# Convolution taps loaded by rows and turned on TensorE, four integer adds moved to GpSimd, and later landings written into the planner

## The chip, the cores and the metric

The kernel runs on one core of a Trainium2 chip. The metric is the device time of one execution in microseconds; the median of three runs stands for the kernel. All times, bytes and clocks below come from those runs and from one profiled execution.

## The reference

Chunked attention feeds a feed-forward block, and that feeds a gated convolution. All of it is computed to fp32 accuracy; the weights and the convolution taps arrive as 64-bit floats (two 32-bit words a number).

```python
# attention inside chunks of 64 tokens, B=8, H=8, S=576, D=64
scores = scale * q_c @ k_c.T;  attn = softmax(scores);  x = attn @ v_c     # -> x: 4608 tokens x 512
# feed-forward with layer norm, 512 -> 2048 -> 512
xn = (x - mu) / sqrt(var + 1e-6) * g_ln
x  = x + relu(xn @ w_ch1) @ w_ch2
# gate: a causal convolution over time with 5 taps a channel
gate_pre[t] = sum over k of conv_w[k] * x[t - 4 + k]
out = (sigmoid(gate_pre) * (x @ w_val)) @ w_out
```

## The kernel before

The 4608 tokens are cut into nine blocks of 512 (`NBLK`), each of four tiles of 128 (`unit(u)`: attention and layer norm of one tile). The feed-forward runs per block, over four groups of 512 hidden columns (`hidden(b, g)`; in the first two blocks `ffn`). Every fp32 product is made of three products of rounded halves (a "high" and a "low" part, the low one being what rounding left). From the third block on, a group is computed with seven products of half-size operands in place of eight (names "1" to "7", line 1241, TensorE tile `m`). The weight operands `late_a` of these are kept in HBM (`a_dram`) and loaded again for each block. At the end the value and output projections follow the same scheme (TensorE tiles `v` and `o`).

**Weights as 64-bit words.** `pieces` turns one or two 512 KB pieces of float64 words into fp32: ScalarE `f32_size` (line 297) and `f32_rest` (line 317), VectorE `f32_upper` (lines 302 and 305) and `f32_join` (line 320, an integer add of 128x1024 words for a pair), and then ScalarE's high part (line 384 or 388) and VectorE's low part (line 393 or 399). The first eight pieces are the weights of group 0. The taps of the convolution, 5 x 512 numbers, take the same route in `conv_taps`; their load reads eight bytes for each of 128 x 20 places, straight into channel-on-partition order.

**The convolution.** For each channel tile, ScalarE multiplies by tap 0 (line 1625, or 1568 for block 0, whose `x` is read back from HBM as `cx` or `late_x`), VectorE adds the other four taps (lines 1632, 1575), and SyncE stores the sum to `gate_dram` (lines 1645, 1587). The sums lie in two halves of `u_room`, so a third sum waits for the first one's store.

**Order of the work.** Nothing is scheduled by the compiler. Each piece of work is an `Op` with an engine, an assumed duration, dependencies and a priority; `Plan.run` plays these through a list scheduler when the kernel is built, and its order is the order in which every engine then executes. An op's result is assumed to be there after a hop, 3500 ns for a DMA, plus the op's own allowance `more`:

```python
HOP = {"PE": 220.0, "DVE": 80.0, "ACT": 80.0, "POOL": 200.0, "SP": 3500.0}
...
a.ready = max(a.ready, end + wait)     # wait holds HOP[e] + op.more
```

When TensorE has nothing ready in the planner's first 60 us, `keep_warm` puts in a 128x128 product of the identity (line 332, tiles `warm_h`, `warm_y`). These are instructions like others: they are executed whether or not the data has come by then. The planner counts 215 ns for one of them (430 ns before 7 us), and the trace shows each as two instructions. All DMAs go through SyncE's queue ("SP"), in planned order.

**Names used below.** `att` is a tile's attention bank on TensorE, `xnt` the turned, normalised tile (line 825 high, line 830 low), `h` and `hh`/`hl` the hidden values, `y` the second product of the feed-forward, `px`/`ps` the probabilities that a transposing DMA turns (line 676), `qT`/`kT` the turned q and k (line 561), `x7d` the operands stored for the value projection (line 1468), `rstd` a [128, 1] reciprocal root on GpSimd (line 756).

Of the kernel before, what the change touches and what calls it, by code (L numbers as in the profile page):

```python
# [18 lines left out]
P = 128  # L19
# [110 lines left out]
def chunk_attention_ffn_gated_conv(  # L130
# [157 lines left out]
    def words(ap):  # L288

        if len(ap.shape) == 3:  # L290
            w = ap.rearrange("p i (n w) -> p i n w", w=2)
            return w[:, :, :, 0], w[:, :, :, 1]
        w = ap.rearrange("p (n w) -> p n w", w=2)
        return w[:, :, 0], w[:, :, 1]
# [21 lines left out]
        lo = words(raw)[0]  # L316
        nc.scalar.activation(out=lo, in_=lo.bitcast(U32), func=AF.Copy, scale=2.0**-29)

    def f32_join(raw, u):
        nc.vector.tensor_tensor(out=u, in0=u, in1=words(raw)[0], op=ALU.add)  # L320

    npiece, uu_n = [0], [0]
    stage, spare = {}, {}
# [11 lines left out]
    def pieces(tags, srcs, pri, keep, dma_pri=None, scale=None, after=None, behind=None):  # L335
# [71 lines left out]
        o_size = add("ACT", 670 * n - 250 * (n - 1), size, [*loads, behind] + room_free, pri)  # L407
        o_rest = add("ACT", 670 * n - 250 * (n - 1), lambda: f32_rest(st["raw"]), [*loads, behind], pri)
        o_up = add("DVE", 1120 * n - 300 * (n - 1), lambda: f32_upper(st["raw"], st["u"]), [o_size], pri)
        o_join = add("DVE", 690 * n - 150 * (n - 1), lambda: f32_join(st["raw"], st["u"]), [o_up, o_rest], pri)  # L410
        if scale is None:
            o_high = add("ACT", 640 * n - 250 * (n - 1), high, [o_join, after], pri)
        else:
# [30 lines left out]
        hold("h0", c)  # L444
        return c

    def conv_taps(pri):

        st, n = {}, KT * KD

        def load():
            st["raw"] = slot("dg1", [P, 2 * n], I32, "cw_raw")
            nc.sync.dma_start(
                out=st["raw"].rearrange("p (n w) -> p n w", w=2),
                in_=conv_w.bitcast(I32).rearrange("k (f p w) -> p (k f) w", p=P, w=2),
            )

        def size():
            st["u"] = cw_sb.rearrange("p k f -> p (k f)").bitcast(I32)
            f32_size(st["raw"], st["u"])  # L460

        a = add("SP", 2000, load, [w_op[0, 2 * KD - 1]], pri)
        b = add("ACT", 200, size, [a], pri)
        c = add("ACT", 200, lambda: f32_rest(st["raw"]), [a], pri)
        d = add("DVE", 400, lambda: f32_upper(st["raw"], st["u"]), [b], pri)
        return add("DVE", 150, lambda: f32_join(st["raw"], st["u"]), [c, d], pri)


    def runs(t):
# [34 lines left out]
    def unit(u):  # L504
# [399 lines left out]
        if u < NT:  # L904
            room = take("qk") + take("uu1")
            early_pri = pri - STEP_TILE
            lq, lk = (
                op("SP", 2640 * len(runs(u)), load_blocks(i), room, p=early_pri) for i in range(2)
            )
            eq = op("DVE", 1110, turn(0), lq, take("A"))  # L910
            ek = op("DVE", 1110, turn(1), lk, take("B"))
            hold("qk", eq, ek)
            ready = [eq, ek]
# [7 lines left out]
        def turned_probabilities():  # L921
            sp = op("ACT", 1250, apart, ex, bu)
            cp = op("SP", 600, crossbar, sp, su, p=pri - 20000.0)
            cp.more = 1000.0
            return op("ACT", 1370, together, cp)

        ep = turned_probabilities() if ready else None
# [370 lines left out]
    def hidden(b, g):  # L1298
# [8 lines left out]
        def product(m, into, new, deps):  # L1307
            rt = RING[ring_n[0] % len(RING)]
            ring_n[0] += 1

            def load():
                w[m] = slot(rt, [P, 2, 2, two_f], F32R, f"a{b}_{g}_{m}")
                nc.sync.dma_start(out=w[m].bitcast(F32), in_=a_dram[g, m].bitcast(F32))

            def go():
                if new:
                    st[into] = bank(tb if into == "b" else ta, f"m{m}_{b}_{g}").rearrange("p (f x) -> p f x", f=2)
                x = operand(m)
                twelve(st[into], lambda s, k: w[m][:, s, k], lambda s, k: x[:, s, k], new)

            at = pri + 1400.0 * MS.index(m)
            ld = add("SP", 1300, load, [a_store[g, m]] + take(rt), at - 16000.0)
            ld.more = 1500.0
            o = add("PE", 1410, go, [ld, B_op[b, m]] + deps, at)
            hold(rt, o)
            if g == NG - 1:
                hold(f"o{m}", o)
            return o
# [228 lines left out]
    def conv_again(f):  # L1557
# [3 lines left out]
        def load():  # L1561
            st["x"] = slot(rt, [P, P0 + NB], F32, f"cx{f}")
            nc.sync.dma_start(out=st["x"][:, P0:], in_=x2_dram[:, f])
            nc.gpsimd.memset(st["x"][:, :P0], 0.0)

        def first():
            st["acc"] = slot(at, [P, XW], F32, f"acc0_{f}")
            nc.scalar.activation(
                out=st["acc"][:, :NB], in_=st["x"][:, :NB], func=AF.Copy, scale=cw_sb[:, 0, f : f + 1]
            )  # L1570
# [18 lines left out]
        pri = when[4 + f, KF // 2]  # L1589
        ox = add("SP", 1300, load, [x2_store[0]] + take(rt), pri - 8000.0)  # L1590
        ox.more = 2500.0
        oa = add("ACT", 740, first, [ox, cw_op] + take(at), pri)
        for i in range(1, KT):
            oa = add("DVE", 760, more(i), [oa], pri)
        hold(rt, oa)
        conv_store[0, f] = add("SP", 728, keep, [oa], pri)
        hold(at, conv_store[0, f])

    def conv(b):
# [19 lines left out]
        for f in range(KD if b else 0):  # L1619
# [31 lines left out]
                oa = add("DVE", 760, more(i), [oa], pri)  # L1651
            last.append(oa)
            conv_store[b, f] = add("SP", 728, keep, [oa], pri)
            hold(at, conv_store[b, f])
        if b == 0:
            x2_store[b] = add("SP", 2900, store, done, pri)
# [358 lines left out]


    g_op = ln_scale()
    for u in range(TB):
        unit(u)
    for g in range(NG):  # L2020
# [4 lines left out]
    for b, f in fstep:  # L2025
# [13 lines left out]
                weight_sums(f // 4)  # L2039
        elif f % 4 == 0:  # L2040
            hidden(b, f // 4)
        if (b, f) == (0, KF // 2 + 1):
            cw_op = conv_taps(when[0, 3 * KF // 4])
        if (b, f) == (NBLK - 1, KF - 4):
            val_weights()
            out_weights()
# [52 lines left out]
```

## Time and profile before

| | |
|---|---|
| three runs | 1072.77, 1078.07, 1076.52 us; median 1076.52 us |
| the profiled execution, its own time | 1073.77 us |
| its span, first to last instruction | 1072.0 us |
| TensorE / VectorE / ScalarE / GpSimd busy | 99% / 80% / 50% / 4% |
| mean granted TensorE clock | 0.998 of 2.4 GHz |
| HBM traffic over the span | 257 GB/s |

TensorE's ends are modelled, so its 99% hides short waits between products. In the first 48 us part of this busy time is the warm-up products.

### The profile page before, as it was taken

The page shows a single profiled execution, that of the slowest core. Times are in us where ns is not written, and L with a number is a line of the kernel's source. Part 1 is how long each engine was busy: PE and PEld are TensorE (multiplying, and loading weights), DVE is VectorE, ACT ScalarE, POOL GpSimd, SP SyncE. Part 2 cuts the span into 40 slices and gives each one's busy share as a digit, 9 for nine tenths or more (in the row PEclk, how much of TensorE's full clock was granted, in tenths as well). Part 3 has the DMA queues.
Part 4 walks back from the last instruction along what each step waited for, and adds up shares of the span by engine and source line. Part 5 has one row for each costly group of instructions (what it writes and reads, how often), then busy time and mean ns, then how long its engine had stood idle before and what let it go on. Part 6 is the DMA issues. An engine that isn't in the chain of part 4 may idle for free.

```text
span 1072.0 us, 22750 instructions
## 1 busy us (share of the span) xinstructions
PE 1056.9 (99%) x8953; PEld 953.9 (89%) x8953; DVE 857.1 (80%) x1463; ACT 539.0 (50%) x871; POOL 42.9 (4%) x81
## 2 busy tenths in 40 slices
PE   9999999999999999999999999999999999999998
PEld 8988878888999988889888889888999999999998
DVE  5989858888876888767888768778766889998785
ACT  5796534445454445444544543554453555655553
POOL 1011100000000000000000000000000000000000
PEclk9999999999999999999999999999999999999999
DMA  8996458666999899899999999899965988999952
GB/s 192 309 339 184 114 130 240 219 199 198 265 361 244 238 311 336 265 258 334 272 265 315 270 241 265 302 266 271 327 229 201 385 328 307 306 337 374 321 206 79
DMA packets 208451, 284.14 MB, mean 265 GB/s; under 512 B 101844, under 2 KB 153560, under 8 KB 208344
## 3 DMA queue, kind: packets, MB, share of 16 engines
q1 hardware_dynamic: 208344, 282.68, 85.1%
q8 instruction: 71, 1.16, 0.5%
q14 instruction: 36, 0.29, 0.1%
HBM read 207.64 MB, written 67.63 MB: 257 GB/s over the span
## 4 chain that ended last, share of the span: by engine, by line
PE 90%; DMA 4%; DVE 3%; ACT 1%; issue 1%; SPq 1%; POOL 0%; DVEq 0%; POOLq 0%; ACTq 0%
PE m L1241 22%; PE o L1241 8%; PE v L1241 8%; PE y L1020 7%; PE yA L1398 4%; PE yB L1398 4%; PE yA L1400 4%; PE yB L1400 4%; PE yA L1399 4%; PE yB L1399 4%; PE att L590 4%; PE att L617 3%; PE h L996 3%; PE h L997 2%; PE h L998 2%; PE warm_h L332 1%
## 5 line engine op out<-in xcount | busy, mean ns | idle before, releaser
L1241 PEld LDWEIGHTS m<-late,late_a 128*128 128x128 f32 x2352 | 297.9, 189 | 22.5 <-DVE c_hl L1340 3.0
L1241 PE MATMUL m<-late,late_a 128*128 128x256 f32 x2352 | 304.7, 280 | 6.2 <-issue 2.2
L1632 DVE SCALAR_TENSOR_TENSOR u_room<-X,cw_sb,u_room 128x516 f32<-128x516 f32 (+1 forms) x128 | 95.4, 749 | 6.3 <-ACT u_room L1625 4.0
L1020 PE MATMUL y<-hh,w 128*128 128x512 f32 x224 | 70.9, 398 | 0.0
L1340 DVE TENSOR_TENSOR c_hh<-c_hh,m 128x512 f32<-128x512 f32 x56 | 38.4, 686 | 38.7 <-ACT c_hh L1333 20.1
L1333 ACT ACTIVATE c_hh<-m 128x512 f32<-128x512 f32 x56 | 33.3, 595 | 58.6 <-PE m L1241 57.9
L1398 PE MATMUL yA<-late_h,w 128*128 128x512 f32 x148 | 59.7, 403 | 0.0
L1398 PE MATMUL yB<-late_h,w 128*128 128x512 f32 x148 | 59.1, 400 | 0.0
L1400 PE MATMUL yA<-late_h,w 128*128 128x512 f32 x148 | 58.2, 393 | 0.6 <-DVE late_h L1371 0.6
L1400 PE MATMUL yB<-late_h,w 128*128 128x512 f32 x148 | 58.1, 393 | 0.0
L1399 PE MATMUL yA<-late_h,w 128*128 128x512 f32 x148 | 57.9, 391 | 0.0
L1399 PE MATMUL yB<-late_h,w 128*128 128x512 f32 x148 | 57.8, 391 | 0.0
L1020 PEld LDWEIGHTS y<-hh,w 128*128 128x128 f32 x224 | 40.9, 188 | 8.5
L996 PE MATMUL h<-xnt,w 128*128 128x512 f32 x112 | 45.6, 407 | 0.0
L1368 ACT ACTIVATE late_h<-c_hh 128x512 fp32r<-128x512 f32 x38 | 23.8, 627 | 42.4 <-DVE c_hh L1340 41.9
L997 PE MATMUL h<-xnt,w 128*128 128x512 f32 x112 | 44.2, 395 | 0.0
L998 PE MATMUL h<-xnt,w 128*128 128x512 f32 x112 | 44.2, 395 | 0.0
L756 POOL TENSOR_TENSOR rstd<-ve,neg_half 128x1 f32<-128x1 f32 x36 | 23.4, 649 | 518.4 <-DVE ve L736 518.1
L1020 PE MATMUL y<-hl,w 128*128 128x512 f32 x112 | 44.0, 393 | 0.0
L685 ACT ACTIVATE pT<-px 128x1024 uint16<-128x1024 uint16 x28 | 38.4, 1372 | 10.9 <-DMA px<-ps 10.8
L1273 ACT ACTIVATE late<-xs 128x512 fp32r<-128x512 f32 x49 | 30.0, 626 | 23.9 <-DVE xs L1267 12.1
L664 ACT ACTIVATE p<-p 128x512 f32<-128x512 f32 x33 | 20.8, 630 | 38.2 <-DVE p L656 21.1
(271 smaller groups left out, 2448.7 us busy)
## 6 DMA issues: line engine op xcount, KB each, us to landing
late_a<-a SPq DMA_DIRECT2D x196, 512.0 KB, 6.0
x7d<-late_x SPq DMA_DIRECT2D x42, 512.0 KB, 5.8
late_a<-x7d SPq DMA_DIRECT2D x39, 512.0 KB, 5.5
raw<-in_moe_w_ch_dram SPq DMA_DIRECT2D x32, 512.0 KB, 8.2
late<-x7d SPq DMA_DIRECT2D x24, 512.0 KB, 5.6
qk_room<-in_q_dram SPq DMA_DIRECT2D x100, 112.0 KB, 5.7
qk_room<-in_k_dram SPq DMA_DIRECT2D x100, 112.0 KB, 4.4
x7d<-x SPq DMA_DIRECT2D x21, 512.0 KB, 6.2
```

Of the source, the lines that this page charges most:

```text
L590: nc.tensor.transpose(ps[:, c], src[:, c], ident)
L685: nc.scalar.activation(out=t.bitcast(U16).rearrange("p (x s) -> p s x", s=2), in_=st["turned"], func=AF.Copy)
L996: nc.tensor.matmul(ps, wh, xh, start=(kk == 0), stop=False)
L997: nc.tensor.matmul(ps, wh, xl, start=False, stop=False)
L998: nc.tensor.matmul(ps, wl, xh, start=False, stop=(kk == KD - 1))
L1020: nc.tensor.matmul(ps, w[:, s], x, start=opens and n == 0, stop=closes and n == 2, skip_group_check=not b)
L1241: nc.tensor.matmul(ps[:, f], l, right(r, k), start=new and f == k == i == 0, stop=k == 1 and i == 2, skip_group_check=True,)
L1340: nc.vector.tensor_tensor(out=st[tag], in0=st[tag], in1=y, op=op)
L1398: nc.tensor.matmul(ps, wh, hh, start=opens and f == 0, stop=False)
L1399: nc.tensor.matmul(ps, wl, hh, start=False, stop=False)
L1400: nc.tensor.matmul(ps, wh, hl, start=False, stop=closes and f == 3)
L1632: nc.vector.scalar_tensor_tensor(out=a, in0=X[b][:, f, i : i + L], scalar=cw_sb[:, i, f : f + 1], in1=a, op0=ALU.mult, op1=ALU.add,)
```

## The change

- The eight pieces of group 0 have their four joins (pairs) on GpSimd, as plain integer tensor adds; the planner counts 2500 ns for one. VectorE keeps all later joins.
- The taps are loaded as 20 rows of 128 numbers (1 KB each), early (priority between the second pair of weights and the second pair of q and k tiles); the four conversion steps work on 20 x 128, TensorE turns the result and VectorE copies it from PSUM to `cw_sb`.
- In `conv_again`, the four zero columns ahead of `cx` are written by ScalarE (identity times 0) in the op that multiplies by tap 0, where GpSimd had a memset of its own.
- The planner's allowance `more` becomes 2500 (from 1000) for the transposing DMA of P, 2500 (from 1500) for loads of `late_a`, 2000 (from 0) for the stores of the gate sums, and 1000 (from 0) for the loads of q and k. This changes the order on all engines from then on; no instruction is added or removed by it.

```diff
-    def f32_join(raw, u):
-        nc.vector.tensor_tensor(out=u, in0=u, in1=words(raw)[0], op=ALU.add)
+    def f32_join(raw, u, by=nc.vector):
+        by.tensor_tensor(out=u, in0=u, in1=words(raw)[0], op=ALU.add)
...
-        o_join = add("DVE", 690 * n - 150 * (n - 1), lambda: f32_join(st["raw"], st["u"]), [o_up, o_rest], pri)
+        if i < 2 * KD:
+            o_join = add("POOL", 1250 * n, lambda: f32_join(st["raw"], st["u"], nc.gpsimd), [o_up, o_rest], pri)
+        else:
+            o_join = add("DVE", 690 * n - 150 * (n - 1), lambda: f32_join(st["raw"], st["u"]), [o_up, o_rest], pri)
...
-    def conv_taps(pri):
+    def conv_taps(load_pri, pri):
...
-            st["raw"] = slot("dg1", [P, 2 * n], I32, "cw_raw")
+            st["raw"] = slot("hl1", [n, 2 * P], I32, "cw_raw")
             nc.sync.dma_start(
-                out=st["raw"].rearrange("p (n w) -> p n w", w=2),
-                in_=conv_w.bitcast(I32).rearrange("k (f p w) -> p (k f) w", p=P, w=2),
+                out=st["raw"], in_=conv_w.bitcast(I32).rearrange("k (f x) -> (k f) x", x=2 * P)
             )
...
+        def tr():
+            st["ps"] = bank("h0", "cw_ps")[:, :n]
+            nc.tensor.transpose(st["ps"], st["u"].bitcast(F32), ident[:n, :n])
+
+        def ev():
+            nc.vector.tensor_copy(cw_sb.rearrange("p k f -> p (k f)"), st["ps"])
...
+            lq.more = lk.more = 1000.0
...
-            cp.more = 1000.0
+            cp.more = 2500.0
...
-            ld.more = 1500.0
+            ld.more = 2500.0
...
-            nc.gpsimd.memset(st["x"][:, :P0], 0.0)
...
+            nc.scalar.activation(out=st["x"][:, :P0], in_=ident[:, :P0], func=AF.Copy, scale=0.0)
...
-        oa = add("ACT", 740, first, [ox, cw_op] + take(at), pri)
+        oa = add("ACT", 1000, first, [ox, cw_op] + take(at), pri)
...
+        conv_store[0, f].more = 2000.0
...
+            conv_store[b, f].more = 2000.0
...
+    cw_op = conv_taps(FIRST + 6.5, FIRST + 9)
...
-        if (b, f) == (0, KF // 2 + 1):
-            cw_op = conv_taps(when[0, 3 * KF // 4])
```

The order on three engines shows the change at the start. First TensorE, where the third and fourth tile of block 0 are turned (`att`) and the second product `y` begins; a warm-up row counts planned ones. Before:

```order
L590 MATMUL att_446<-ident,W_4_W_5_151 128x128 x4
L590 MATMUL att_446<-ident,W_1_W_2_159 128x128 x4
L332 MATMUL warm_y<-ident 128x128 x14
L590 MATMUL att_486<-ident,W_6_W_7_152 128x128 x4
L590 MATMUL att_486<-ident,W_6_W_7_158 128x128 x4
L332 MATMUL warm_y<-ident 128x128 x17
L1084 MATMUL h_10_807<-xnt_0_465,w_442 128x256 x6
L1084 MATMUL h_10_807<-xnt_1_466,w_539 128x256 x6
```

And now:

```order
L605 MATMUL att_459<-ident,W_4_W_5_151 128x128 x4
L605 MATMUL att_459<-ident,W_1_W_2_159 128x128 x4
L1100 MATMUL h_01_579<-xnt_1_472,w_588 128x256 x3
L332 MATMUL warm_y<-ident 128x128 x16
L605 MATMUL att_500<-ident,W_6_W_7_152 128x128 x4
L605 MATMUL att_500<-ident,W_6_W_7_158 128x128 x4
L332 MATMUL warm_y<-ident 128x128 x2
L1131 MATMUL y_0_793<-hh_00_694,w_757 128x256 x2
L1131 MATMUL y_0_793<-hl_00_708,w_757 128x256
L1131 MATMUL y_0_793<-hh_00_694,w_757 128x256 x2
L1131 MATMUL y_0_793<-hl_00_708,w_757 128x256
```

The first `y` has come ahead of the first `h` of the second half, and 18 planned warm-ups stand there where there were 31. Over the whole program the planned warm-ups go from 96 to 81.

Next ScalarE, where the second pair of weights (`raw_339`, in `qk_room`) is taken up, while the first pair's high part (`w`) waits for its join. Before:

```order
L693 ACTIVATE W_4_W_5_157<-att_280 128x512
L297 ACTIVATE qk_room<-raw_339 128x1024
L388 ACTIVATE w_442<-u_room,g_sb 128x512 x2
L317 ACTIVATE raw_339<-raw_339 128x1024
L825 ACTIVATE xnt_0_465<-att_236 128x2x128
L825 ACTIVATE xnt_1_466<-att_236 128x2x128
```

And now:

```order
L708 ACTIVATE W_4_W_5_157<-att_280 128x512
L297 ACTIVATE cw_rows<-cw_raw 20x128
L317 ACTIVATE cw_raw<-cw_raw 20x128
L388 ACTIVATE w_422<-u_room,g_sb 128x512 x2
L297 ACTIVATE qk_room<-raw_339 128x1024
L317 ACTIVATE raw_339<-raw_339 128x1024
L840 ACTIVATE xnt_0_471<-att_236 128x2x128
L840 ACTIVATE xnt_1_472<-att_236 128x2x128
```

The two steps on the taps' words stand ahead of the first pair's high part, of the second pair's two steps and of the first tile's `xnt`.

Last GpSimd, from its first root on (the rows ahead are constants and memsets). Before:

```order
L756 TENSOR_TENSOR rstd_409<-ve_383,neg_half 128x1
L585 MEMSET v_452 128x8
L756 TENSOR_TENSOR rstd_457<-ve_430,neg_half 128x1
L756 TENSOR_TENSOR rstd_677<-ve_640,neg_half 128x1
L756 TENSOR_TENSOR rstd_736<-ve_709,neg_half 128x1
```

And now:

```order
L320 TENSOR_TENSOR u_room<-u_room,raw_249 128x1024
L771 TENSOR_TENSOR rstd_419<-ve_385,neg_half 128x1
L600 MEMSET v_464 128x8
L771 TENSOR_TENSOR rstd_469<-ve_444,neg_half 128x1
L320 TENSOR_TENSOR qk_room<-qk_room,raw_339 128x1024
L771 TENSOR_TENSOR rstd_678<-ve_645,neg_half 128x1
L320 TENSOR_TENSOR u_room<-u_room,raw_575 128x1024
L771 TENSOR_TENSOR rstd_750<-ve_729,neg_half 128x1
L320 TENSOR_TENSOR qk_room<-qk_room,raw_583 128x1024
```

The four joins stand between the four roots of block 0. Further on, the four memsets of line 1564 are gone from this queue, one of `cx` and three of `late_x`.

## Rows read from the trace of the kernel before

**Rows 1.** The page: span, busy time by engine, and the granted clock in forty slices.

```profile
span 1072.0 us, 22750 instructions
PE 1056.9 (99%) x8953; PEld 953.9 (89%) x8953; DVE 857.1 (80%) x1463; ACT 539.0 (50%) x871; POOL 42.9 (4%) x81
```

**Rows 2.** TensorE's groups by line (busy us, mean ns | idle before): the two warm-up groups.

```profile
...
L332 PE MATMUL warm_h<-ident 128*128 128x128 f32 x116 | 17.0, 298 | 1.5 <-POOL ident masks.py:199 1.5
...
L332 PE MATMUL warm_y<-ident 128*128 128x128 f32 x76 | 9.1, 275 | 0.0
...
```

**Rows 3.** The chain of waits near the start: start us, us, what.

```profile
...
43.98 3.80 PE warm_y L332 x34
...
```

**Rows 4.** VectorE's timeline between 18 and 48 us: start us, us, instruction.

```profile
...
18.00 1.22 DVE L320 CUSTOM_DVE_ANT_0 u_room<-raw,u_room 128x2048 uint16<-128x2048 uint16 x1
...
36.92 1.23 DVE L305 SCALAR_TENSOR_TENSOR u_room<-raw,u_room 128x1024 int32<-128x1024 int32 x1
...
43.00 1.22 DVE L320 CUSTOM_DVE_ANT_0 u_room<-raw,u_room 128x2048 uint16<-128x2048 uint16 x1
...
46.66 1.22 DVE L393 TENSOR_TENSOR w<-u_room,w 128x1024 fp32r<-128x1024 f32 x1
...
```

**Rows 5.** ScalarE's timeline at 18 us; in brackets its idle time before.

```profile
...
18.60 1.16 ACT L297 ACTIVATE qk_room<-raw 128x1024 f32<-128x1024 f32 x1 [2.47 <-DMA raw<-in_moe_w_ch_dram]
...
```

**Rows 6.** GpSimd by line and shape over the whole span: its one wide operation.

```profile
...
L812 POOL COPY X<-xs 128x512 f32<-128x512 f32 x13 | 9.4, 746 | 105.8 <-DVE t L1440 81.7 <-ACT h L1368 14.6 <-ACT xs L806 9.5
...
```

**Rows 7.** GpSimd's timeline in the first 41 us: two reciprocal roots.

```profile
...
18.16 1.46 POOL L756 TENSOR_TENSOR rstd<-ve,neg_half 128x1 f32<-128x1 f32 x1 [16.76 <-DVE ve L736]
...
40.92 0.55 POOL L756 TENSOR_TENSOR rstd<-ve,neg_half 128x1 f32<-128x1 f32 x1 [3.63 <-DVE ve L736]
...
```

**Rows 8.** The tile of the convolution's words: duration ns min/median/max, start.

```profile
...
L453 SPq DMA_DIRECT2D cw_raw<-in_moe_conv_w_dram x1: 3827/3827/3827, 66.7 to 66.7; - x1
L297 ACT ACTIVATE cw_sb<-cw_raw x1: 202/202/202, 76.6 to 76.6; 128x20 f32<-128x20 f32 x1
...
```

**Rows 9.** What TensorE waited for, whole span: us in total, times, longest.

```profile
...
PE m L1241 <- issue: 2.2, 1, 2.2
PE m L1241 <- ACT c_hl L1333: 1.5, 1, 1.5
...
PE att L590 <- DVE xn L775: 1.3, 1, 1.3
PE m L1241 <- DMA late_a<-a: 1.0, 1, 1.0
PE m L1241 <- DVE c_hl L1340: 1.0, 1, 1.0
PE yA L1400 <- DVE late_h L1371: 0.6, 1, 0.6
```

**Rows 10.** The chain of waits from 390 us on: its transfers.

```profile
...
391.32 4.29 DMA late_a<-a
...
529.07 3.65 DMA px<-ps
...
552.31 5.47 DMA gd<-u_room
...
591.95 8.27 DMA x7d<-late_x
...
```

**Rows 11.** Around 690 us: VectorE's variance, GpSimd's next two instructions, VectorE's normalisation.

```profile
...
689.64 0.15 DVE L736 TENSOR_SCALAR ve<-mv 128x1 f32<-128x1 f32 x1
...
693.41 0.10 POOL L1564 MEMSET cx<- 128x4 f32 x1 [11.65 <-DMA x7d<-x]
693.53 0.55 POOL L756 TENSOR_TENSOR rstd<-ve,neg_half 128x1 f32<-128x1 f32 x1
...
694.11 0.55 DVE L775 TENSOR_SCALAR xn<-x,mv,rstd 128x512 f32<-128x512 f32 x1 [2.45 <-POOL rstd L756]
...
```

**Rows 12.** Busy time of each engine in a stretch, clock, DMA share, GB/s.

```profile
...
626.00:632.00 6.00, 5.27 (x26) 4.72 (x27) 2.16 (x5) 2.83 (x4) 0.00 (x0) 0.72 1.10 230
...
```

More of the change, by code (lines that the diff above doesn't have):

```diff
@@ L445, in ln_scale @@
         return c
-    def conv_taps(pri):
+    def conv_taps(load_pri, pri):
         st, n = {}, KT * KD
         def load():
-            st["raw"] = slot("dg1", [P, 2 * n], I32, "cw_raw")
+            st["raw"] = slot("hl1", [n, 2 * P], I32, "cw_raw")
             nc.sync.dma_start(
-                out=st["raw"].rearrange("p (n w) -> p n w", w=2),
-                in_=conv_w.bitcast(I32).rearrange("k (f p w) -> p (k f) w", p=P, w=2),
+                out=st["raw"], in_=conv_w.bitcast(I32).rearrange("k (f x) -> (k f) x", x=2 * P)
             )
         def size():
-            st["u"] = cw_sb.rearrange("p k f -> p (k f)").bitcast(I32)
+            st["u"] = slot("hh1", [n, P], I32, "cw_rows")
             f32_size(st["raw"], st["u"])
[L462 to L466, printed above, removed]
+        def tr():
[3 more added lines that the diff above has]
+            nc.vector.tensor_copy(cw_sb.rearrange("p k f -> p (k f)"), st["ps"])
+        a = add("SP", 60, load, take("hl1"), load_pri)
+        b = add("ACT", 250, size, [a] + take("hh1"), pri)
+        c = add("ACT", 250, lambda: f32_rest(st["raw"]), [a], pri)
+        d = add("DVE", 330, lambda: f32_upper(st["raw"], st["u"]), [b], pri)
+        e = add("DVE", 200, lambda: f32_join(st["raw"], st["u"]), [c, d], pri)
+        f = add("PE", 70, tr, [e] + take("h0"), pri)
+        g = add("DVE", 80, ev, [f], pri)
+        hold("hl1", e)
+        hold("hh1", f)
+        hold("h0", g)
+        return g
     def runs(t):
```

## Prediction

> **What bounds the kernel now.** I read the page first: TensorE is busy for 1056.9 of 1072.0 us, VectorE for 80% [rows 1]. So only time in which TensorE does nothing useful can be won, unless its work shrinks, and no edit takes products away. The groups by line show the first kind of such time: warm-up products of the identity, 116 + 76 = 192 instructions in the first 48 us [rows 2]. In the chain of waits 34 of them take 3.80 us [rows 3], 0.112 us each, so all 192 are worth about 21.5 us. The list of waits shows the second kind: six rows with 7.6 us in all, 2.2 + 1.5 + 1.3 + 1.0 + 1.0 + 0.6 [rows 9]. After the 2.2 us one the granted clock averages 0.72 over 6 us [rows 12]: a share of 0.56 of that stretch, 3.4 us, at the lower of the two levels (1.2 GHz), so 1.7 us of work lost. Everything that this change can win lies in about 21.5 + 7.6 + 1.7 = 31 us. The rest is products back to back.
>
> **The joins.** A join of a pair takes 1.22 us on VectorE [rows 4], so four leave VectorE 4.9 us. What they are worth is read where the warm-ups stand. The third pair's upper part ended at 36.92 + 1.23 = 38.15 us, but its join began only at 43.00, as VectorE had other work ahead of it; its low part ended at 46.66 + 1.22 = 47.88 [rows 4]. TensorE's last warm-ups ran from 43.98 to 47.78 [rows 3]. On GpSimd the join can begin when the upper part ends, since by the order only a root stands between it and the join before it.
>
> How long it takes there no row shows. The nearest one is GpSimd's copy of 128x512, one input, 746 ns [rows 6]. Twice the elements give 1.5 us as a lower bound. Twice the elements and a second input read in turn give 3.0 us as an upper bound. I take 2.4 us, nearer to the upper end, because the add has two inputs. Then the third join ends at 40.6 in place of 44.2, and the low part, with a high part and a low part of about 1.1 and 1.2 us behind it and short queues, at 43 to 44 us. That is 4 us before TensorE stopped warming up. What hides a GpSimd join is the rest of the start, 38 to 43 us; a join that outlasts this is paid by TensorE.
>
> The order agrees: 81 planned warm-ups in place of 96 are 30 instructions fewer, 30 x 0.112 = 3.4 us. This is what the executed order gives back if the data keeps up with it.
>
> While GpSimd adds, VectorE's two-input instructions may have to wait. A row bears on this: a root of 128x1 takes 0.55 us at 40.92, but 1.46 us at 18.16, when VectorE's join runs from 18.00 to 19.22 [rows 4, 7]. The Trainium skill has this as a rule (SBUF — State Buffer, section "Who interferes with whom"): a VectorE instruction with two SBUF inputs, or in a two-port mode, and a GpSimd instruction that reads SBUF shut each other out, whichever comes second waiting for the whole of the first. The trace agrees, by the two roots. In the new order it bites once: the fourth join begins about when VectorE turns to the next pair's shift and upper part, which would wait up to 2.4 us less what VectorE does before, 0.7 us: 1.7 us on VectorE, of which I charge 0.3 us to TensorE, since the weights behind it are wanted some microseconds later.
>
> The Trainium skill gives a price for this add (GPSIMD Engine Reference, section "3.1 Elementwise — side-by-side cycle accounting"): 4497 ns for 2048 fp32 elements, so half of it, 2.25 us, is an estimate for one join; by it the sum would be the same within 0.3 us.
>
> **The taps.** Their load held SyncE for 3.83 us at 66.7 us [rows 8], with TensorE busy; taking it away there is worth nothing I can point to, 0 to -0.5 us. The new load of 20 rows stands right behind the second pair of weights, and what is queued behind another transfer lands after it. ScalarE had waited 2.47 us for that pair, until 18.60 [rows 5]. So the taps come at 18.6 us or later, and ScalarE, whose queue now has them ahead of the first pair's high part and of the second pair, does two steps of 0.2 us [rows 8] there first. Behind them wait the first tile's `xnt` and, through it, the attention bank that TensorE wants next. TensorE itself has a turn of 128x20 in its order (0.2 us, an estimate from the two 0.2 us steps), and stands still until the taps are there. I charge 0.2 us for the turn and 0.3 us for the lateness; ScalarE's later gap takes up the rest. Bounds: 0 and 1.2 us.
>
> Start in all: -3.4 + 0.3 + 0.2 + 0.3 = **-2.6 us**, between -3.6 and +1.5 (joins of 3.0 us on both later pairs, 2 x 0.6, and the upper bounds of lock and taps).
>
> **The zero columns.** At 689.64 us VectorE has the variance; the root that follows on GpSimd begins at 693.53, as the memset of `cx` ahead of it waited for the store of `x7d` to free its room until 693.41; VectorE's normalisation idles 2.45 us [rows 11], and TensorE 1.3 us [rows 9]. Without the memset the root can start at 689.8. ScalarE's clear waits for the load of the same room, as did ScalarE's first tap before, so nobody new is held up. **-1.3 us**, 0 at worst (the time can go to another wait).
>
> **The allowances.** They move no work, only its place. Four waits of TensorE have chains through what they touch: 1.5 us behind the turned P (3.65 us transfer at 529.07), 1.0 us behind a `late_a` load (4.29 us at 391.32), 0.6 us behind a gate sum that waited for the store of an earlier one (5.47 us at 552.31), and 1.0 us behind a turn of q that came in between [rows 9, 10]. All four: -4.1 us; I take the last by half: -3.6 us. But this order is new from start to end, and it will have waits of its own. Of the old 7.6 us, 2.2 us had none of these causes but SyncE standing for an 8.27 us store at 591.95 [rows 10], and that pattern is still in the order. I leave these 2.2 us and their clock loss in, and add 1.5 us for new waits, about a fifth of the old total. **-2.1 us**, between -6.5 (the 2.2 us go as well) and +4 (a second wait of 2.2 + 1.7 us).
>
> **Sum.** -2.6 - 1.3 - 2.1 = -6.0 us: 1073.8 - 6.0 = 1067.8 us beside the profiled execution. Its own time lies 2.7 us under the median of the runs shown (1076.5), which spread over 5.3 us. I put the forecast near the middle between both, at **1069 us**. Differences under 0.5% (5.4 us) are about what a measurement of this kernel can't tell from no change.
>
> **The rivals.**
> - *The start gives nothing.* The joins take 3 us or more, or hold VectorE at several places, or the taps hold ScalarE. For it: the 1.46 us root [rows 7], two inputs of words at every second place. Against it: 4 us of room at the third pair. Time: 1069 + 2.6 = 1071.6.
> - *The waits come back elsewhere.* A new order has as many late transfers as the old one; DMA engines are as loaded as before. For it: the 8.27 us store is untouched [rows 10]. Against it: four allowances are raised to what the rows show. Time: 1069 + 3.4 (or 2.1 + 1.3) = 1072.4.
> - *Slower: the join is far longer on GpSimd.* Each microsecond over 2.4 is paid at the second pair (ScalarE's high part stands ahead of the probabilities' eviction) and again at the third: 2 us for 1. The change loses from 2.4 + 6.0 / 2 = 5.4 us a join on; at 8 us it is 1069 + 11.2 = 1080. Against it: the upper bound by the copy row is 3.0 us.
> - *More than forecast.* The 2.2 us wait goes with its 1.7 us of clock, and no new one comes: 1069 - 5.4 = 1063.6.
>
> **How the numbers follow.** Forecast 0.47, start nothing 0.15, waits back 0.18, slower 0.08, more 0.12. Faster by over 0.5% (under 1071.1) holds the forecast with nine tenths and "more": 0.54, and a fifth of the two rivals near the line, 0.07: 0.61. Slower by over 0.5% (over 1081.9): most of the slow rival, and as much of runs that scatter, together 0.09. Within: 0.30. The range reaches from the fast end of "more" with the scatter, 1060, to a little over the two middle rivals with it, 1078; it leaves out the slow rival and the tails, 2 in 10.
>
> **What would show each step.** A join on GpSimd between 1.5 and 3.0 us, and no VectorE row over 2 us beside it; the first `y` at 43 to 45 us with 162 warm-up instructions; the taps' ScalarE step at 18.6 to 19.2; GpSimd's roots after 300 us starting within 0.3 us of the variance; no wait of TensorE over 1 us on P, `late_a` or gate stores. The prediction is wrong if a join takes over 4 us, if TensorE idles over 2 us in the first 50, or if waits of TensorE sum to over 7 us again.

## The result, and the profile after

The changed kernel is slower: 1080.64 us median against 1073.4 us of the kernel before in the same series, ratio 1.0062, 95% interval 1.0047 to 1.0078. The prediction was 1069 us, faster, in a range from 1060 to 1078. All ratios below are to the kernel before, run beside the kernel named.

The page of the changed kernel, span and engines (answers to [rows 1]):

```profile
span 1082.2 us, 22674 instructions
PE 1059.7 (98%) x8924; PEld 953.6 (88%) x8924; DVE 854.4 (79%) x1460; ACT 540.0 (50%) x875; POOL 51.4 (5%) x81
```

The two profiled executions lie further apart than the medians (7.2 us): their spans are 1072.0 and 1082.2 us. Three places in the program show where these 10.2 us arise: the start of the first `y` product, of the first late product `m`, and of the first product `v` (first starts, from the views of these tiles).

| | first `y` | first `m` | first `v` | end |
|---|---|---|---|---|
| before | 49.0 | 244.4 | 880.0 | 1072.0 |
| after | 47.9 | 245.7 | 889.4 | 1082.2 |

So the start still leads by 1.1 us at the first `y`, where 4 to 6 were forecast; that is lost at 244 us, and the stretch from 245.7 to 889.4 takes 643.7 us in place of 635.6: 8.1 of the 10.2 us.

What TensorE waited for in the changed kernel (us in total, times, longest; answers to [rows 9]):

```profile
PE att L632 <- DMA v<-in_v_dram: 4.3, 2, 3.6
PE m L1257 <- DMA late_a<-a: 4.1, 1, 4.1
PE m L1257 <- DVE c_hl L1356: 2.0, 2, 1.2
PE cw_ps L466 <- DVE cw_rows L320: 1.7, 1, 1.7
...
PE m L1257 <- ACT c_hl L1349: 1.7, 2, 1.3
...
PE y L1131 <- DVE w L393: 0.7, 1, 0.7
```

The 1.3 us behind `xn` are gone, and so are the waits behind the turned P near 536 us and behind `late_a` near 396, and the 2.2 us one that the prediction had left in; but single waits of 3.6, 4.1 and 1.7 us are new, and each of these three is followed by a lower clock. Windows of the changed kernel (us, busy time of PE, PEld, DVE, ACT and POOL, granted clock, DMA share, GB/s):

```profile
20.00:26.00 6.00, 5.27 (x32) 5.24 (x33) 4.58 (x12) 4.32 (x7) 0.75 (x2) 0.72 0.84 153
422.00:440.00 18.00, 17.20 (x153) 15.71 (x154) 14.10 (x26) 7.85 (x14) 0.55 (x1) 0.91 1.02 338
546.00:560.00 14.00, 12.87 (x124) 11.43 (x125) 8.90 (x18) 4.63 (x9) 0.55 (x1) 0.88 0.88 251
```

A mean of 0.72 over 6 us is 3.4 us at the lower level (1.2 GHz), 1.7 us of work lost; the other two are 2 x 0.09 x 18 = 3.2 and 2 x 0.12 x 14 = 3.4 us at it, 1.6 and 1.7 us lost. The six rows of waits make 14.5 us against 7.6, and the clock 1.7 + 1.6 + 1.7 = 5.0 against 1.7: 10.2 us more in all. Against them stand 30 warm-ups fewer (3.4 us), so these rows account for 6.8 of the 10.2 us between the spans. Some 3 us more are in no row: TensorE's busy time grew by 2.8 us (1056.9 to 1059.7), where clock and warm-ups alone would leave it as it was.

**The joins** took about the time forecast. GpSimd's timeline in the changed kernel:

```profile
16.18 2.39 POOL L320 TENSOR_TENSOR u_room<-u_room,raw 128x1024 int32<-128x1024 int32 x1 [14.77 <-DVE rs L723]
...
40.75 2.63 POOL L320 TENSOR_TENSOR u_room<-u_room,raw 128x1024 int32<-128x1024 int32 x1 [0.99 <-DVE u_room L305]
...
49.36 2.46 POOL L320 TENSOR_TENSOR qk_room<-qk_room,raw 128x1024 int32<-128x1024 int32 x1 [4.82 <-DVE qk_room L305]
```

The prediction took 2.4 us, and the third join begins 2.2 us earlier than VectorE's did [rows 4]. Beside the fourth, VectorE's next shift takes 2.54 us:

```profile
47.28 0.69 DVE L302 TENSOR_SCALAR qk_room<-qk_room 128x1024 int32<-128x1024 int32 x1
...
49.83 2.54 DVE L302 TENSOR_SCALAR u_room<-u_room 128x1024 int32<-128x1024 int32 x1
```

2.54 - 0.69 = 1.85 us of standing still, where the prediction had 1.7. The 0.7 us of `y` behind `w` may be its echo: such a row is in all eight kernels below in which a shift meets a join, and in none without.

**The taps** took longer than forecast. The changed kernel around 20 us, by time:

```profile
14.60 0.37 SPq L456 DMA_DIRECT2D cw_raw<-in_moe_conv_w_dram  x1
...
19.38 0.31 ACT L297 ACTIVATE cw_rows<-cw_raw 20x128 f32<-20x128 f32 x1 [3.27 <-DMA cw_raw<-in_moe_conv_w_dram]
...
20.40 0.28 DVE L320 CUSTOM_DVE_ANT_0 cw_rows<-cw_raw,cw_rows 20x256 uint16<-20x256 uint16 x1
20.73 0.13 PEld L466 LDWEIGHTS cw_ps<-ident,cw_rows 20*128 20x128 f32 x1 [1.92 <-DVE cw_rows L320]
20.73 0.23 PE L466 MATMUL cw_ps<-ident,cw_rows 20*128 20x20 f32 x1 [1.73 <-DVE cw_rows L320]
```

Issued at 14.60, behind the weights, they reach ScalarE at 19.38; two steps there and three on VectorE take until 20.73, 1.35 us more; TensorE stands 1.73 us and then runs at the lower clock.

**The middle**, at the 4.1 us wait. SyncE's planned order there, before and after, around the same turned P (`px_6279` and `px_6290`):

```
L577 DMA v_6197<-in_v_dram 64x4x64 x4
L1313 DMA late_a_0_2_2145<-a_4_192 128x1024
L1587 DMA gd_75<-u_room 128x512
L549 DMA qk_room<-in_q_dram 32x4x224 x4
L676 DMA_TRANSPOSE px_6279<-ps_6261 128x8x128
L549 DMA qk_room<-in_k_dram 32x4x224 x4
L1313 DMA late_a_0_2_2145<-a_2_193 128x1024
```

```
L1603 DMA gd_75<-u_room 128x512
L1329 DMA late_a_0_2_2256<-a_4_192 128x1024
L564 DMA qk_room<-in_q_dram 32x4x224 x4
L592 DMA v_6238<-in_v_dram 64x4x64 x4
L564 DMA qk_room<-in_k_dram 32x4x224 x4
L691 DMA_TRANSPOSE px_6290<-ps_6261 128x8x128
L1329 DMA late_a_0_2_2256<-a_2_193 128x1024
```

The loads of v and k have come to stand between those of q and the turned P. SyncE's timeline there, before:

```profile
526.38 2.58 SPq L549 DMA_DIRECT2D qk_room<-in_q_dram  x4
529.07 1.26 SPq L676 DMA_TRANSPOSE px<-ps  x1
530.38 2.01 SPq L549 DMA_DIRECT2D qk_room<-in_k_dram  x4
532.49 2.29 SPq L1313 DMA_DIRECT2D late_a<-a  x4
```

and after:

```profile
530.60 6.59 SPq L592 DMA_DIRECT2D v<-in_v_dram  x4
537.28 1.97 SPq L564 DMA_DIRECT2D qk_room<-in_k_dram  x4
539.36 1.27 SPq L691 DMA_TRANSPOSE px<-ps  x1
540.73 2.99 SPq L1329 DMA_DIRECT2D late_a<-a  x4
```

What SyncE waited for in the changed kernel between 528 and 548 us, first row:

```profile
SPq L592 <- DMA late_a<-a: 4.2, 3, 1.9
```

Four v loads, which take 2.62 us to issue where nothing holds them (at 697.69 us before), take 6.59 here, as three of them wait for earlier `late_a` transfers. The turned P goes out 10.3 us later than before (529.07 and 539.36), and the `late_a` loads behind it 8.2 us later (532.49 and 540.73), for which TensorE stands 4.1 us at 547. The kernel as a whole ran some 5 to 7 us late here, by the count of products done; the rest is the new order.

### The profile page after: what moved, and what is told of

It reads as the page before. It is cut to its first block, busy times and chain, and to the rows that moved or that the text cites. A ratio compares the mean times of both kernels' runs of the same rounds, so it can differ in the third digit from the quotient of the medians.

```text
span 1082.2 us, 22674 instructions
## 1 busy us (share of the span) xinstructions
PE 1059.7 (98%) x8924; PEld 953.6 (88%) x8924; DVE 854.4 (79%) x1460; ACT 540.0 (50%) x875; POOL 51.4 (5%) x81
## 4 chain that ended last, share of the span: by engine, by line
PE 80%; DMA 10%; DVE 3%; SPq 2%; issue 2%; ACT 2%; POOL 0%; DVEq 0%; ACTq 0%; POOLq 0%
PE m L1257 22%; PE o L1257 8%; PE v L1257 8%; PE y L1036 6%; PE yA L1414 4%; PE yB L1414 4%; PE yA L1416 4%; PE yB L1416 4%; PE yB L1415 4%; PE yA L1415 4%; PE att L632 3%; PE att L605 3%; DMA raw<-in_moe_w_ch_dram 2%; PE h L1012 2%; PE h L1014 2%
## 5 line engine op out<-in xcount | busy, mean ns | idle before, releaser
L1036 PE MATMUL y<-hh,w 128*128 128x512 f32 x224 | 71.6, 401 | 0.0
L576 DVE STREAM_TRANSPOSE kT<-qk_room 128x512 f32<-128x512 f32 x28 | 30.5, 1091 | 10.8 <-DMA qk_room<-in_k_dram 10.8
```

Source lines behind the costliest of these rows:

```text
L1036: nc.tensor.matmul(ps, w[:, s], x, start=opens and n == 0, stop=closes and n == 2, skip_group_check=not b)
```

## The experiments

Theory A: the early taps cost several us, since their load lands late. Theory D: the raised allowances cost, by the order of SyncE. Rival B: any order drawn anew costs, whatever drew it. Rival C: a lead of the start is taken back by transfers of the middle. (The expectation of `e1_allow` calls D "theory A", and some call the rivals theories; theory B in `f2_fixed_order` and `f4_hybrid` is that the edits give what was forecast and a redrawn order takes it back.)

**One part alone.** Each kernel holds one part of the diff shown above: `e1_allow` its four `more` lines, `e2_joins` the hunk with `by=nc.vector` and the one with `add("POOL", ...)`, `e3_taps` the new `conv_taps` with its call, `e4_clear` the `memset` hunk with the 1000 ns. The cores of the four:

```diff
+            lq.more = lk.more = 1000.0
...
-            cp.more = 1000.0
+            cp.more = 2500.0
```
```diff
+            o_join = add("POOL", 1250 * n, lambda: f32_join(st["raw"], st["u"], nc.gpsimd), [o_up, o_rest], pri)
```
```diff
+    cw_op = conv_taps(FIRST + 6.5, FIRST + 9)
```
```diff
-            nc.gpsimd.memset(st["x"][:, :P0], 0.0)
...
+            nc.scalar.activation(out=st["x"][:, :P0], in_=ident[:, :P0], func=AF.Copy, scale=0.0)
```

> The four raised allowances alone on the kernel before (1 in place of 0 us on the loads of q and k, 2.5 for 1 on the turned P, 2.5 for 1.5 on late_a, 2 for 0 on the stores of the convolution). Theory A (the allowances make the new waits of the middle: a v load that lands at 422.7, a late_a load at 547): 4 to 9 us slower than before, with single waits of TensorE over 2 us between 390 and 700 us that before did not have. Rival B (any new order draws its waits anew, and the early part of the change drew these): 0 to 4 us faster, the old waits behind P, late_a and the gate stores gone, and no new one over 2 us.

Measured 1.0054 (1.0035 to 1.0073). SyncE has the same order around the turned P, and TensorE waits 3.7 us for `late_a` there. A second wait is of another kind:

```profile
PE att L590 <- DVE xn L775: 6.4, 3, 3.4
PE m L1242 <- DMA late_a<-a: 4.6, 2, 3.7
```

Without the clear on ScalarE the memset still holds GpSimd's root, as in [rows 11]. That the allowances cost, as theory D has it, stands.

> The four joins on GpSimd alone. Theory A (the early taps spoil the start, not the joins): the first y begins 3 to 4 us earlier than before (at about 44 us), granted clock 1.0 over the first 45 us, and 2 to 4 us faster in all if the middle draws no new wait. Rival (the joins on GpSimd hold up VectorE or the high parts): the first y at 47 us or later, no gain. If the middle is drawn anew by any change of the start (rival B), the gain at 50 us is there and is lost between 390 and 700 us.

Measured 0.9989 (0.9969 to 1.0009). The first `y` begins at 43.9 us, 5.1 earlier than before, and at the first `y` of full width (512 columns) 1.6 of it are left (71.6 and 73.2). At the first `m` (242.3) it leads by 2.1, at the first `v` (881.3) it is 1.3 behind, with 3.1 us of waiting for `xn` at 694: the lead is lost in the middle. In the end no gain that can be told from none.

> The early taps with their turn on TensorE alone, no other edit. Theory A: TensorE waits about 1.7 us for the turned rows at 20.7 us, the granted clock falls to about 0.6 over the 4 us behind it, and the first y begins 3 to 4 us later than before; 3 to 5 us slower in all, more or less by what the middle draws. Rival (the wait is taken up by the warm-ups, and the late start of the changed kernel comes from its joins): first y within 1 us of before, no change in time.

Measured 1.0058 (1.0039 to 1.0076), but not as theory A had it: TensorE waits for no turned rows, the first `y` is 0.6 us late, and the loss comes later (first `m` 247.8, first `v` 890.3). With the old joins more warm-ups are executed (198 in place of 162), and the taps are there in time; that the redrawn order made the loss is what is left, and not shown. The rival had that right, and the time wrong.

> The clear of four columns on ScalarE in place of GpSimd's memset alone, with the 1000 ns that the planner takes for the step. The forecast: root on GpSimd within 0.3 us of the variance near 690 us, TensorE's wait of 1.3 us there gone, about 1.3 us faster, up to 2. Rival: the 260 ns more in the planner's cost move the order, and the time changes by up to 3 us either way, with the waits of the middle at other places.

Measured 1.0027 (1.0010 to 1.0044). The wait behind `xn` is gone, and a longer one has come 8 us behind it. In that kernel TensorE's longest wait, from the list of its waits:

```profile
PE m L1241 <- ACT c_hl L1333: 4.6, 2, 3.2
```

ScalarE's step ahead of this `c_hl`, from its timeline:

```profile
700.68 1.35 ACT L685 ACTIVATE pT<-px 128x1024 uint16<-128x1024 uint16 x1 [3.27 <-DMA px<-ps]
```

and the transfer that this step waited for, from the chain of waits between 690 and 704 us:

```profile
694.21 6.45 DMA px<-ps
```

SyncE still waits 6.6 us for a store to free the room of `cx` (6.5 before), and the turned P stands behind that load in the queue. It goes out earlier than before (694.21 and 695.54), but its transfer takes 6.45 us in place of 4.0, so ScalarE gets it at 700.68 (699.61 before), and there TensorE waits for what it has gained, and more. Why the transfer was longer is not shown.

**The order held fixed.** The planner's order of the kernel before is written out as a list of steps and followed on every engine.

```diff
-        for op in self.ops:
-            op.left = len(op.deps)
...
+        for i in range(0, len(b), 2):
+            n = int.from_bytes(b[i : i + 2], "big") - 1
+            if n < 0:
+                self.idle()
+            else:
+                self.ops[n].fn()
```

> A control: the kernel before with its own order written out as a list, the same instructions in the same places. Ratio 1.000 within its interval of about 0.002. Its profile is a second execution of the kernel before: it shows which waits of the middle come at the same place with the same length in each execution (expected: all six, within 1 us each).

Measured 0.9997 (0.9979 to 1.0014). But the waits do not repeat to 1 us. The same kernel's waits in this execution, beside [rows 9]:

```profile
PE att L609 <- DVE xn L794: 2.5, 1, 2.5
PE m L1260 <- DMA late_a<-a: 2.0, 2, 1.3
PE m L1260 <- issue: 1.7, 1, 1.7
```

1.3 became 2.5 at the normalisation, 1.0 became 2.0, 2.2 became 1.7. One execution fixes a wait to about 1 us, no better; the six waits of [rows 9] are samples.

> The planned order of the kernel before, written into the kernel as a list and kept on every engine; in it the four joins stand at their old places but on GpSimd, the columns are cleared by ScalarE, and the last 15 planned warm-ups (30 instructions) are left out. No other step moves. Theory B (the edits give what was forecast, and the redrawn order takes it back): the first y 3 to 4 us earlier, the waits of the middle where the kernel before has them, the 1.3 us near 694 us gone, and 3 to 5 us faster in all. Rival C (the gain of the start is absorbed later even in the same order, since what paces the rest is transfers): first y earlier, but 0 to 1.5 us faster in all, with the lead shrinking between 50 and 400 us.

Measured 1.0028 (1.0010 to 1.0046): theory B's forecast for it fell. With 30 warm-ups fewer in the old order TensorE stood 1.3 us for `xnt`, with a clock of 0.73 between 44 and 50 us, and the first `y` began at 49.5: in that order the joins did not set it. So the joins bring `y` forward only together with an order drawn for them. In the middle, waits for `late_a` took 3.5 us and for `c_hl` 3.5; the longest, 2.9 us at 702.5, stands where that of `e4_clear` does.

> As the run with the fixed order, and in it the early taps as in the changed kernel: their load behind the second pair of weights, their four steps and their turn at the places that they have there. Theory A (the taps wait for their load and TensorE for them, with a fallen clock behind it): 2 to 4 us slower than the fixed order without them, a wait of 1 to 2 us for the turned rows near 20.7 us, granted clock near 0.6 over the 4 us behind it. Rival (in this order warm-ups cover the wait, as they did where the early taps came alone): within 1 us of the fixed order without them.

Measured 1.0061 (1.0039 to 1.0083), 0.33% or 3.5 us over the fixed order without the taps. Its first row of waits:

```profile
PE cw_ps L485 <- DVE cw_rows L342: 3.5, 1, 3.5
```

and its window behind that:

```profile
20.00:26.00 6.00, 5.02 (x32) 4.98 (x33) 4.79 (x13) 3.40 (x5) 0.00 (x0) 0.72 0.83 151
```

Theory A stands where the taps are waited for.

> Joins on GpSimd alone, with an order written out as a list: up to 75 us the order that the planner gave the joins alone (162 warm-ups; there TensorE was 1.7 us ahead at 73 us), behind it the remaining steps in the order of the kernel before. Theory B (a redrawn middle took the lead back): the lead of about 1.7 us stands to the end, ratio 0.997 to 0.999. Theory C (transfers pace the middle, and a lead ends at the next of them): the lead is gone by 400 us or by 700, ratio 0.9995 to 1.002.

Measured 1.0017 (0.9995 to 1.0038). The first `y` at 43.9, the first `m` at 245.6, later than before (244.4): the lead is gone before the middle begins, at `xnt` (2.0 us) near 81 us. The time is as theory C has it, but the lead went 6 us behind the seam between the two orders (75 us), so the seam can be the cause as well.

**Numbers of the planner without work behind them.**

```diff
-        o_join = add("DVE", 690 * n - 150 * (n - 1), ...
+        o_join = add("DVE", 740 * n - 150 * (n - 1), ...
```

> The kernel before with one number of the planner changed, no instruction added or taken away but two planned warm-ups: a join on VectorE planned at 740 in place of 690 ns a piece. It moves 416 of 2554 rows of TensorE and 72 of 630 of SyncE. Theory B (an order drawn anew is some us slower than the one of the kernel before, whatever drew it): 2 to 8 us slower. Rival (an order drawn anew is as good on average, and the loss comes from the early taps and the allowances): within 2 us.

Measured 0.9999 (0.9977 to 1.0020). Rival B falls as a rule: a widely redrawn order can be as good.

```diff
-            cp.more = 1000.0
+            cp.more = 1200.0
```

> The kernel before with one number of the planner changed: the allowance behind the turned P is 1.2 in place of 1.0 us. It moves 94 of 2554 rows of TensorE and 21 of 630 of SyncE, all in the middle. Theory B: 1 to 5 us slower, with a wait of TensorE over 2 us at a place where before has none. Rival: within 1.5 us, or faster, as the longer allowance is nearer to the transfer's time.

Measured 1.0057 (1.0032 to 1.0081): 0.2 us in one allowance costs 6 us.

> The kernel before with one allowance of the four raised: 2.5 in place of 1.0 us behind the turned P. With 1.2 us the kernel was 0.57% slower. If this allowance makes the loss of the four: ratio 1.004 to 1.007. Rival (each value draws its own order): anything from 0.999 to 1.006, without relation to the 1.2 us case.

(`cp.more = 2500.0` alone.) Measured 1.0056 (1.0037 to 1.0075).

> The kernel before with one allowance of the four raised: 2.0 in place of 0 us on the stores of the convolution. It moves 155 places of VectorE's and 68 of SyncE's order, more than any other single edit here. If this allowance makes the loss: ratio 1.004 or more. If it does what it is planned for: the wait of 0.6 us at 562.9 gone and ratio 0.998 to 1.000.

(`conv_store[...].more = 2000.0` at both places, alone.) Measured 1.0068 (1.0044 to 1.0092). The wait at 562.9 is gone, but `xn` is waited for four times, 6.6 us in all. Either of the two alone makes a loss as large as that of all four. It is not made at the place traced above: between 530 and 550 us TensorE waits 1.0 us at most in these two and in `r3_p_cost`.

**The two losses undone in the changed kernel.**

```diff
-    cw_op = conv_taps(FIRST + 6.5, FIRST + 9)
+    cw_op = conv_taps(FIRST + 0.7, FIRST + 9)
```

> The changed kernel with one number changed: the load of the taps stands behind the load of the four rows of g, ahead of the weights, in place of behind the second pair of weights. The order of every engine is that of the changed kernel but for the start (turn of the taps behind the turn of g; 164 warm-ups in place of 162). Theory A (the taps cost 3.5 us because they land late): no wait for the turned rows over 0.6 us, granted clock 1.0 between 20 and 26 us, and 2.5 to 4 us faster than the changed kernel, so a ratio of 1.002 to 1.004 to the kernel before. Rival (the start is paced by VectorE and the joins, or the lead is taken back in the middle): ratio 1.005 or more.

Measured 1.0018 (0.9999 to 1.0037), 0.44% or 4.7 us better than the changed kernel. The taps are turned at 7.6 us, nobody waits for them, the clock between 20 and 26 us is 1.00, and the first `y` begins at 44.4. Theory A is shown; its 2.5 to 4 us were a little low. The allowances are still raised here, and SyncE still sends v and k ahead of the turned P, but TensorE waits 2.1 us there (for `kT`, at 540), and neither the 3.6 nor the 4.1 us wait is on the list:

```profile
PE att L632 <- ACT late L1289: 2.3, 1, 2.3
PE m L1257 <- ACT c_hl L1349: 2.2, 1, 2.2
PE m L1257 <- DVE kT L576: 2.1, 1, 2.1
```

So these two waits belong to one kernel's timing; what the allowances cost comes back as others.

> The changed kernel without its four raised allowances (joins, early taps and column clear stay). Theory D (the allowances cost 5 to 6 us also beside the other edits, by the order of SyncE: loads of v that wait stand ahead of the late_a load that TensorE wants): a ratio of 0.999 to 1.002 to the kernel before, no wait for late_a over 2.5 us near 540, but the wait for the taps near 20 us still there. Rival (any redrawn middle costs as much): ratio 1.005 or more.

Measured 0.9989 (0.9970 to 1.0007), 0.73% or 7.8 us better than the changed kernel. The turned P stands behind the q loads again, and no wait for `late_a` is on the list. The wait for the taps is there, but the clock did not fall. Row of waits, and window:

```profile
PE cw_ps L466 <- DVE cw_rows L320: 1.8, 1, 1.8
```

```profile
20.00:26.00 6.00, 5.13 (x45) 5.10 (x46) 5.32 (x16) 5.55 (x10) 1.04 (x2) 1.00 0.83 155
```

> The changed kernel with both undone parts mended: the taps' load ahead of the weights (as in t1_taps_first) and no raised allowance (as in e5_no_allow). Its order is that of e5_no_allow but for the start. If the two losses add (4.4 us by the taps, 7.8 us by the allowances in the changed kernel): ratio 0.994 to 0.996, faster than both kernels. Rival C (a lead of the start is taken back at a transfer of the middle): ratio 0.998 to 1.000, as e5_no_allow.

(Both edits: `FIRST + 0.7`, and no `more` line raised.) Measured 0.9957 (0.9937 to 0.9978), 1070.01 against 1075.09 us: faster than both kernels. The losses add. Its largest waits between 240 and 880 us, in place of 3.6 and 4.1 us:

```profile
PE m L1256 <- DVE h L1386: 2.2, 1, 2.2
PE m L1256 <- DVE hl L1023: 1.4, 1, 1.4
PE m L1256 <- ACT c_hl L1348: 1.2, 2, 0.7
```

First `y` 44.5, first `m` 240.9, first `v` 875.4: the middle takes 634.5 us (635.6 before), and the lead of the start is kept, against rival C.

> As b1_first_noallow without the clear on ScalarE (memset on GpSimd as before). The clear alone was 0.27% slower, with the 1.2 us gained near 693 lost again near 702: if that holds in this order, ratio 0.2 to 0.3% under that of b1. Rival (what the clear alone cost was the planner's 260 ns more, a redrawn order): within 0.2% of b1.

(b1 with the `memset` on GpSimd.) Measured 0.9969 (0.9946 to 0.9993): the clear is worth 0.12%, 1.3 us, in this order, the size forecast, but the two intervals overlap. By `e4_clear` the expectation had the kernel without the clear faster; it is not, and the rival held. The 260 ns of the plan go back with the clear, so the order is not quite the same.

One thing the list of waits shows in every trace: TensorE waits for VectorE's `xn` in all eleven kernels with the memset on GpSimd (1.3 to 6.6 us in all), and in none of the nine with the clear on ScalarE.

> As b1_first_noallow with the four joins on VectorE as before (taps loaded first, clear on ScalarE, no raised allowance; 188 warm-ups in place of 164). If the joins give what was forecast for them (3.4 us of warm-ups, at least 2 us of it kept): ratio 0.997 to 0.999, 2 to 3 us slower than b1. Rival (the lead of the start is taken back at the transfers near 88 us, where b1 lost 1.5 us of it): within 1 us of b1.

(b1 with `add("DVE", ...)` for all joins.) Measured 0.9971 (0.9947 to 0.9995): 0.14%, 1.5 us, for the joins, again within the intervals, and between the 2 to 3 us of the forecast and the 1 us of its rival. In the profiles the joins lead by 5.1 us at the first `y` (44.5 and 49.6) and by 2.1 at the end (spans 1068.1 and 1070.2).

> As b1_first_noallow with two of the four allowances raised as in the changed kernel: 1.0 us on the loads of q and k, 2.5 us on late_a; those on the turned P and on the stores of the convolution stay as before. With all four the same kernel is 0.6% slower. If P and the stores make that loss (each alone on the kernel before cost 0.6 to 0.7%): ratio within 0.2% of b1. Rival (every raised allowance redraws the order of SyncE and costs some us): 0.999 or more.

(b1 with `lq.more = lk.more = 1000.0` and `ld.more = 2500.0`.) Measured 1.0122 (1.0090 to 1.0155), 1.65% or nearly 18 us worse than b1, the worst of all, and worse than with all four (t1, 1.0018). Its longest waits:

```profile
PE m L1257 <- ACT c_hl L1349: 7.0, 3, 3.9
PE m L1257 <- DMA late_a<-a: 3.0, 1, 3.0
```

So the loss can't be put down to two of the four. Each set draws an order of its own, and how good it is does not go with how much is raised.

## Why the prediction was wrong

The sum was -2.6 (start), -1.3 (columns), -2.1 (allowances), -6.0 us in all; measured were +6.7 (0.62%). Of these 12.7 us the allowances make some 9 to 10, the taps 3 to 4, and the joins 1 to 1.6. The sign "waits of TensorE sum to over 7 us again" came true (14.5).

- **The allowances are the step that failed, in sign.** "They move no work, only its place" was right, and the four waits with chains through them did go, with the 2.2 us that the prediction left in. But "I ... add 1.5 us for new waits, about a fifth of the old total" took the rest of the order for as good as it was. Taking them out is worth 7.8 us (e5 against the changed kernel) or 6.5 (b1 against t1, 0.61%), each to some 3 us by the intervals: the term was +6.5 to +7.8, beyond its bound of +4. The rival of waits that come back elsewhere named the mechanism and its place (transfers), but priced it at the two gains lost (2.1 + 1.3 = 3.4 us): a new order that is worse than the old one was in no rival.
- **The taps were mis-sized.** The prediction charged 0.5 us, lateness within 0 and 1.2. It saw when they land (18.6 or later; ScalarE began at 19.38) and who waits, but counted two steps of 0.2 us behind that, and not VectorE's three steps and the hops: 1.35 us from ScalarE's start to the turn. (Its premise that what is queued behind another transfer lands after it was right only roughly: the last load of the weights ahead, issued at 14.1, landed 5.3 us later, no sooner than ScalarE began on the taps.) It had the clock's price for the middle [rows 12], but not here, where TensorE stands 1.7 us. Measured: 4.7 us by moving the load ahead, 3.4 by b1 against e5, 3.5 by f3 against f2.
- **The joins were right at the start:** price, order, lock, and a first `y` at 43 to 45 us, which the joins alone (43.9), t1 (44.4) and b1 (44.5) show. (The lock's 1.7 us on a step of 0.7 make a row of 2.4, so the sign "no VectorE row over 2 us" did not fit the prediction's own term.) The estimate that the Trainium skill gave (GPSIMD Engine Reference, section "3.1 Elementwise — side-by-side cycle accounting"), 2.25 us, is 5 to 15% under the 2.38 to 2.64 us of the traces, and the measurement decides. The Trainium skill's rule on the two engines (SBUF — State Buffer, section "Who interferes with whom") fits the shift of 2.54 us if that shift ran in a two-port mode, which no trace shows: it ended 0.55 us after the join. What is kept to the end is 1.5 us by the ratios and 2.1 by the spans, half to two thirds of the 3.1 us of the sum (3.4 less 0.3), which the intervals can't tell from all of it. They bring this only with an order drawn for them: in the old order (f2) the first `y` came at 49.5.
- **The zero columns were right in place:** in none of the kernels with the clear does TensorE wait for VectorE's `xn`. Whether the 1.3 us stay hangs on what is late next: alone they were lost at the turned P behind the load of `cx` on SyncE; by b1 and b2 they seem to stay. "Nobody new is held up" was true; that TensorE would now come earlier to the next transfer was left out.
- Without the allowances, and with the taps' lateness at nothing, the same sum gives -2.6 - 0.3 - 1.3 = -4.2 us, a ratio of 0.9961; b1 measured 0.9957. Part of this agreement is luck: the runs give 1.5 us for the joins, where the sum has 3.1, and 1.3 for the clear, so that nearly 2 of b1's 4.6 us have no term; b4, with no join moved, is already 3.1 us faster than the kernel before. It is within the intervals.
- Two bounds don't come out of their terms: the start's upper one is -2.6 + 1.2 + 1.4 + 0.9 = +0.9, not +1.5, and the allowances' lower one -2.1 - 2.2 - 1.7 = -6.0, not -6.5. Neither changes which step failed.

What stays open: why the clock fell behind the 1.7 us wait of the changed kernel and not behind the 1.8 us of e5, with much the same start; through which waits the allowances cost in each order, of which one was followed to its cause; and what in a planned order tells a good one from a bad one ahead of its run.

## What to carry to other kernels

A number that a planner uses is an edit to the whole order: 0.2 us in one allowance cost 6 us, and a term for it should be a spread, not the sum of the waits it aims at. Here the spread lay to the slow side: of five kernels that changed nothing but numbers of the planner (r2, r3, e1, s_p, s_cs), one was as fast as the kernel before and four were 0.54 to 0.68% slower. A transfer that a start waits for is placed by when its last consumer must run, with every step between counted; ahead of the large loads nobody waited for this one, behind them it cost 3.4 to 4.7 us. And where a wait is taken away, ask which queue holds the next one.

## What the runs showed of the hardware

GpSimd's add of words, 128x1024 with one input at every second place, took 2.38 to 2.64 us in all runs with it. A VectorE shift of words with a single input took 2.51 to 2.54 us in place of 0.69 when it met one, in each of the eight kernels with the planner's own order of the joins, so it is not two-input instructions alone that stand still. A wait of 1.7 us was followed by 3.4 us at the lower clock (1.2 GHz) in the changed kernel, and one of 1.8 us by none in e5. The transfer of a turned P took 4.0 us in one kernel and 6.45 in another (before and e4). The same instructions in the same order had waits that differ by up to 1.2 us between two executions.
